# Late weights of a fused attention and two-MoE kernel: the bit operations of the float64 decode work in a PSUM bank instead of in place in SBUF

## Chip, cores and metric

The kernel runs on one core of a Trainium2 chip. The metric is the device time of one execution in microseconds (us). PE or TensorE is the matrix engine, DVE or VectorE, ACT or ScalarE, POOL or GpSimd and SP or SyncE are the others; SP issues the transfers here.

## What is computed

```python
# attention in chunks of 64 positions: batch 8, 8 heads, 576 positions, head dim 64
scores = scale * np.matmul(q_c, k_c.transpose(0, 1, 2, 4, 3))
scores = scores - np.max(scores, axis=-1, keepdims=True)
attn = np.exp(scores)
attn = attn / (np.sum(attn, axis=-1, keepdims=True) + 1e-09)
out = np.matmul(attn, v_c)
...
x = attn_out.transpose(0, 2, 1, 3).reshape(4608, 512)
h = x @ w_in                                # first MoE, 512 -> 2048 -> 512
x = (h * (1.0 / (1.0 + np.exp(-h)))) @ w_out
...
h = x @ w_in                                # second MoE, 512 -> 1024 -> 512
e = np.exp(h - np.max(h, axis=-1, keepdims=True))
solu = h * (e / (np.sum(e, axis=-1, keepdims=True) + 1e-09))
mu = np.mean(solu, axis=-1, keepdims=True)
var = np.mean((solu - mu) ** 2, axis=-1, keepdims=True)
out = ((solu - mu) / np.sqrt(var + 1e-06) * g_ln) @ w_out
```

## The kernel before

The 4608 tokens go through in nine blocks of 512. Each number is held as a pair of float16 values, a high part and the low rest, and a product of two such pairs is three matmuls into one PSUM bank. The helper `split` makes a pair: ScalarE writes the high part (L110), VectorE (L115) or GpSimd (L114) the low one. Blocks 0 and 1 use plain products (`h_group`, `x_part`, `m_h`, `m_out`), while the weights are still being decoded; later blocks use a scheme of seven products for each two-by-two block of operands (`h_fast`, `x_fast`, `m_fast`), whose operands `w1_sums` and `w2_sums` form from the weights during block 1 (lines 391 to 406).

The weights lie in DRAM as float64, that is as pairs of 32-bit words (tile `wst`). There are 48 of 128 x 512: numbers 0 to 31 are the first MoE's, 32 to 39 the second MoE's input weights `w3q`, 40 to 47 its output weights `w4h` and `w4l`. Each is decoded in three steps. `dec_scale` (L129, ScalarE) scales the high word as a float into a tile; `dec_bits` (VectorE) shifts the result left by 3 (L136), puts in three bits of the low word (L137) and the sign (L139); `dec_split` makes the pair, with GpSimd's low split for numbers up to 39 and VectorE's for 40 to 47. The order in which steps are handed over is

```python
    def weights(n=1):
        for _ in range(n):
            d3()
            d1()
            d2()
```

with `d1` the scaling of one weight, `d2` the bit operations and `d3` the split of an earlier one. Numbers below `SB = 32` are scaled into a PSUM bank `wp`, and only the last bit operation writes an SBUF tile `wy`. The 16 late weights, 32 to 47, are scaled straight into `wy` and worked on in place; they have two such buffers (pool `two`, tag `o`), so a scaling waits until the split of the weight two before has read its buffer. `NW1` and `NX1` say after which groups of block 1 `weights` is called.

All PSUM tiles come from one pool, `ps1`, of eight banks with one tag, taken in turn: hidden groups (`h_ps`, L362 to L364), attention scores and outputs (`s_ps`, `x_ps`), sums of weights (`wq`), `m_h`'s two banks (`h2_ps`, shown in traces as h_ps), and `wp`. A scheduler orders each engine's instructions by priority when the program is built; each engine then runs its own list in order. `m_h` of block 0 runs four times in block 1, before hidden groups 5, 7, 9 and 11, and `m_norm` follows it (L763 exp, L765 the product e, L771 square).

Of the kernel before, what the change touches and what calls it, by code (L numbers as in the profile page):

```python
# [10 lines left out]
I32 = mybir.dt.int32  # L11
AF = mybir.ActivationFunctionType
ALU = mybir.AluOpType
# [3 lines left out]
P = 128  # L17
# [29 lines left out]
def fused(ctx: ExitStack, tc: tile.TileContext, qkv, w1, w2, w3, w4, g_ln, out):  # L47
    nc = tc.nc
    V, A, G, T = nc.vector, nc.scalar, nc.gpsimd, nc.tensor
# [27 lines left out]
    ps1 = ctx.enter_context(tc.tile_pool(name="ps1", bufs=8, space=PSUM))  # L77
# [6 lines left out]
    for d in range(KD):  # L84
        for f in range(4):
            if f % 2 == 0:
                tag = f"w2_{2 * d + f // 2}" if d < 3 else f"q{12 + f // 2}"
                y = one.tile([P, 2, 2, 4, P], F16, tag=tag, name="w2t")
# [42 lines left out]
    def dec_bits(c, y):  # L131
        st, p, wh, wl, gain = c
        c[1] = y
        if y is None:
            c[1] = y = p
        V.tensor_scalar(out=p, in0=p, scalar1=3, scalar2=None, op0=ALU.logical_shift_left)  # L136
        V.scalar_tensor_tensor(out=p, in0=st[:, :, 0], scalar=29, in1=p,  # L137
                               op0=ALU.logical_shift_right, op1=ALU.bitwise_or)
        V.scalar_tensor_tensor(out=y, in0=st[:, :, 1], scalar=-2 ** 31, in1=p,  # L139
                               op0=ALU.bitwise_and, op1=ALU.bitwise_or)  # L140
# [228 lines left out]
    def g_split(b, f, eng_h=V):  # L369
        return split(*g_of(b, f), graw.pop(f), S_G, eng_h, V)  # L370
# [471 lines left out]
    for k in range(KD):  # L842
        for n in range(2):
            y = w3q[n, k // 2]
# [30 lines left out]
    def d2():  # L875
        if mid:
            i, c = mid.pop(0)
            dec_bits(c, ytile(i) if i < SB else None)
            out_.append((i, c))
            if at[0] < 36 or len(raw) + len(mid) < 2:  # L880
                fetch()
# [47 lines left out]
    for b in range(NB):  # L929
# [4 lines left out]
        for f in range(K1):  # L934
            if b < FAST:
# [10 lines left out]
                else:  # L946
                    y = g_split(b, f, A)
# [124 lines left out]
```

## Time and profile before

| | before |
|---|---|
| median of 3 runs | 1187.79 us (1187.39 to 1190.37) |
| profiled execution, its own time | 1187.17 us |
| its span | 1185.4 us |
| mean granted clock of TensorE | 0.986 |
| busy: TensorE, VectorE | 1130.4 us, 913.3 us |
| busy: ScalarE, GpSimd | 802.7 us, 250.6 us |

The span runs from the first to the last instruction of the profiled execution; its own time is a little longer. Busy shares are means over the whole span. Times of the trace below are microseconds from the start of the span.

### The profile page before, as it was taken

The page shows a single profiled execution, that of the slowest core. Times are in us where ns is not written, and L with a number is a line of the kernel's source. Part 1 is how long each engine was busy: PE and PEld are TensorE (multiplying, and loading weights), DVE is VectorE, ACT ScalarE, POOL GpSimd, SP SyncE. Part 2 cuts the span into 40 slices and gives each one's busy share as a digit, 9 for nine tenths or more (in the row PEclk, how much of TensorE's full clock was granted, in tenths as well). Part 3 has the DMA queues.
Part 4 walks back from the last instruction along what each step waited for, and adds up shares of the span by engine and source line. Part 5 has one row for each costly group of instructions (what it writes and reads, how often), then busy time and mean ns, then how long its engine had stood idle before and what let it go on. Part 6 is the DMA issues. An engine that isn't in the chain of part 4 may idle for free.

```text
span 1185.4 us, 23577 instructions
## 1 busy us (share of the span) xinstructions
PE 1130.4 (95%) x9036; PEld 767.9 (65%) x9036; DVE 913.3 (77%) x1638; ACT 802.7 (68%) x1475; POOL 250.6 (21%) x243
## 2 busy tenths in 40 slices
PE   5989998998999999999999999999999999999998
PEld 4434443444557866787678767876787777777863
DVE  5889999578587797789878986888689868886453
ACT  6787677775577667756875687568755875587243
POOL 2545424334201520031003100310021002100001
PEclk8989998999999999999999999999999999999999
DMA  7878554543346655777566667666777666655704
GB/s 276 269 233 253 176 180 107 161 145 123 125 116 196 187 178 153 187 206 196 160 187 198 195 159 196 196 197 160 170 216 203 160 161 213 179 161 133 208 25 115
DMA packets 205169, 209.18 MB, mean 176 GB/s; under 512 B 120192, under 2 KB 130432, under 8 KB 205056
## 3 DMA queue, kind: packets, MB, share of 16 engines
q1 hardware_dynamic: 205056, 207.68, 61.5%
q8 instruction: 70, 1.15, 0.4%
q14 instruction: 43, 0.35, 0.1%
HBM read 156.24 MB, written 24.12 MB: 152 GB/s over the span
## 4 chain that ended last, share of the span: by engine, by line
PE 52%; DVE 19%; ACT 11%; DMA 8%; issue 6%; POOL 2%; SPq 0%; ACTq 0%; POOLq 0%; DVEq 0%
PE o_ps L813 4%; PE o_ps L820 4%; PE o_ps L812 4%; PE pa L593 3%; PE pa L592 3%; PE pa L591 3%; PE pa L490 3%; DVE vbl L115 3%; PE pa L492 3%; PE pa L491 3%; DMA vs<-qkv 2%; DMA wst<-w 2%; DMA qk<-qkv 2%; PE pa L707 2%; DVE wy L139 2%
## 5 line engine op out<-in xcount | busy, mean ns | idle before, releaser
L110 ACT ACTIVATE q<-hc 128x512 f16<-128x512 f32 x196 | 119.1, 624 | 41.6 <-DVE hc L578 16.4
L115 DVE SCALAR_TENSOR_TENSOR q<-hc,q 128x512 f16<-128x512 f32 x196 | 138.2, 721 | 6.6 <-ACT q L110 5.1
L114 POOL TENSOR_TENSOR qbl<-qk,qbh 64x512 f16<-64x512 f32 x54 | 71.4, 1323 | 265.0 <-ACT qbh L110 222.6
L591 PE MATMUL pa<-q,ring 128*128 128x256 f16 x448 | 122.2, 273 | 0.0
L593 PE MATMUL pa<-q,ring 128*128 128x256 f16 x448 | 122.2, 273 | 0.0
L592 PE MATMUL pa<-q,ring 128*128 128x256 f16 x448 | 122.2, 273 | 0.0
L812 PE MATMUL o_ps<-w4h,uT 128*128 128x512 f16 x288 | 109.3, 380 | 0.3 <-ACT o L824 0.3
L813 PE MATMUL o_ps<-w4l,uT 128*128 128x512 f16 x288 | 109.3, 379 | 0.0
L778 POOL TENSOR_TENSOR c<-c,mhalf 128x2 f32<-128x2 f32 (+1 forms) x22 | 14.1, 640 | 393.1 <-DVE c L777 385.4
L491 PEld LDWEIGHTS <-ring 128*128 128x128 f16 x784 | 76.6, 98 | 19.6 <-issue 9.2
L592 PEld LDWEIGHTS <-ring 128*128 128x128 f16 x784 | 76.7, 98 | 11.1
L591 PEld LDWEIGHTS <-ring 128*128 128x128 f16 x784 | 76.6, 98 | 11.1
L490 PEld LDWEIGHTS <-ring 128*128 128x128 f16 x784 | 76.6, 98 | 10.5
L593 PEld LDWEIGHTS <-ring 128*128 128x128 f16 x784 | 76.6, 98 | 9.0
L492 PEld LDWEIGHTS <-ring 128*128 128x128 f16 x784 | 76.6, 98 | 9.0
L820 PE MATMUL o_ps<-w4h,uT 128*128 128x512 f16 x288 | 70.2, 379 | 0.0
L490 PE MATMUL pa<-x,ring 128*128 128x256 f16 x224 | 61.1, 273 | 7.7 <-ACT hc L512 5.0
L490 PE MATMUL pa<-xb,ring 128*128 128x256 f16 x224 | 61.1, 273 | 0.0
L491 PE MATMUL pb<-x,ring 128*128 128x256 f16 x224 | 61.1, 273 | 0.0
L492 PE MATMUL pb<-x,ring 128*128 128x256 f16 x224 | 61.1, 273 | 0.0
L492 PE MATMUL pa<-x,ring 128*128 128x256 f16 x224 | 61.1, 273 | 0.0
L591 PE MATMUL pb<-q,ring 128*128 128x256 f16 x224 | 61.1, 273 | 0.0
(277 smaller groups left out, 3493.1 us busy)
## 6 DMA issues: line engine op xcount, KB each, us to landing
ring<-w1s SPq DMA_DIRECT2D x196, 256.0 KB, 3.4
ring<-w2s SPq DMA_DIRECT2D x196, 256.0 KB, 3.6
wst<-w SPq DMA_DIRECT2D x48, 512.0 KB, 4.7
qk<-qkv SPq DMA_DIRECT2D x29, 512.0 KB, 3.7
vs<-qkv SPq DMA_DIRECT2D x36, 256.0 KB, 3.2
out<-o SPq DMA_DIRECT2D x36, 256.0 KB, 2.3
w1s<-ws SPq DMA_DIRECT2D x32, 128.0 KB, 1.7
w2s<-ws SPq DMA_DIRECT2D x16, 256.0 KB, 2.0
```

The source lines that it names most:

```text
L110: A.activation(dst_h, src, AF.Copy, scale=scale)
L114: return G.tensor_tensor(out=dst_l, in0=src, in1=dst_h, op=ALU.subtract).ins
L115: return V.scalar_tensor_tensor(out=dst_l, in0=src, scalar=scale, in1=dst_h, op0=ALU.mult, op1=ALU.subtract).ins
L490: T.matmul(ps[:, c], wh, x[:, 0, k], start=first, stop=False, skip_group_check=True)
L491: T.matmul(ps[:, c], wh, x[:, 1, k], start=False, stop=False, skip_group_check=True)
L492: T.matmul(ps[:, c], wl, x[:, 0, k], start=False, stop=k == 1, skip_group_check=True)
L591: T.matmul(ps[:, c], wh, g[:, 0], start=first, stop=False, skip_group_check=True)
L592: T.matmul(ps[:, c], wh, g[:, 1], start=False, stop=False, skip_group_check=True)
L593: T.matmul(ps[:, c], wl, g[:, 0], start=False, stop=q == 1 and f == 3, skip_group_check=True)
L812: T.matmul(ps, uh[:, k], w4h[:, k, :], start=k == 0, stop=False)
L813: T.matmul(ps, uh[:, k], w4l[:, k, :], start=False, stop=False)
L820: T.matmul(ps, ul[:, k], w4h[:, k, :], start=False, stop=k == K2 - 1)
```

## The change

For a late weight the shift now reads the SBUF tile that ScalarE has scaled, and writes a PSUM bank taken at this point, behind the scaling. The second operation works in that bank, and the third reads it and writes the same SBUF tile as before. These are 16 more PSUM tiles, one for each weight from 32 to 47. Weights below 32 are decoded as before. Lines behind 135 move down by two: L136, L137 and L139 become L138, L139 and L141, and `m_h`'s matmuls L663 become L665.

```diff
     def dec_bits(c, y):
         st, p, wh, wl, gain = c
         c[1] = y
+        s = p
         if y is None:
-            c[1] = y = p
-        V.tensor_scalar(out=p, in0=p, scalar1=3, scalar2=None, op0=ALU.logical_shift_left)
+            c[1] = y = s
+            p = ps1.tile([P, 512], I32, tag="mm", name="wp")
+        V.tensor_scalar(out=p, in0=s, scalar1=3, scalar2=None, op0=ALU.logical_shift_left)
         V.scalar_tensor_tensor(out=p, in0=st[:, :, 0], scalar=29, in1=p,
                                op0=ALU.logical_shift_right, op1=ALU.bitwise_or)
         V.scalar_tensor_tensor(out=y, in0=st[:, :, 1], scalar=-2 ** 31, in1=p,
                                op0=ALU.bitwise_and, op1=ALU.bitwise_or)
```

The order of TensorE's instructions is the same in both programs. Those of ScalarE and VectorE differ only where late weights are decoded. ScalarE, at the last attention tile of block 1, before (`wy_1386` is weight 32, `wy_1396` 33, `wy_1403` 34, `wy_1522` 35; `vbh` is the high part of v):

```order
L110 ACTIVATE x2_2_1432<-x2_ps_1329 128x512
L110 ACTIVATE vbh_115<-vs_1325 64x8x64 x2
L110 ACTIVATE x_1179<-x_ps_1435 128x4x128
L129 ACTIVATE wy_1396<-wst_1372 128x512
L110 ACTIVATE w3q_104<-wy_1386 128x512
L129 ACTIVATE wy_1403<-wst_1382 128x512
L110 ACTIVATE w3q_106<-wy_1396 128x512
L129 ACTIVATE wy_1522<-wst_1392 128x512
L110 ACTIVATE w3q_104<-wy_1403 128x512
L110 ACTIVATE x_1179<-x_ps_1493 128x4x128
```

and with the change, where `wy_1404` is weight 34 and `wy_1524` 35:

```order
L110 ACTIVATE x2_2_1434<-x2_ps_1329 128x512
L129 ACTIVATE wy_1396<-wst_1372 128x512
L110 ACTIVATE w3q_104<-wy_1386 128x512
L129 ACTIVATE wy_1404<-wst_1382 128x512
L110 ACTIVATE vbh_115<-vs_1325 64x8x64 x2
L110 ACTIVATE x_1179<-x_ps_1437 128x4x128
L110 ACTIVATE w3q_106<-wy_1396 128x512
L129 ACTIVATE wy_1524<-wst_1392 128x512
L110 ACTIVATE vbh_115<-vs_1466 64x8x64
L110 ACTIVATE x_1179<-x_ps_1495 128x4x128
```

The split of v stands behind the scalings of weights 33 and 34 now, where it stood ahead of both.

VectorE, around the bit operations of weight 40, before (`wy_1647` is weight 40, `wy_1656` 41; `g` is a hidden group's low half):

```order
L136 TENSOR_SCALAR wy_1647<-wy_1647 128x512
L137 SCALAR_TENSOR_TENSOR wy_1647<-wst_1625,wy_1647 128x512
L139 SCALAR_TENSOR_TENSOR wy_1647<-wst_1625,wy_1647 128x512
L115 SCALAR_TENSOR_TENSOR g_1642<-g_1640,g_1642 128x512
L136 TENSOR_SCALAR wy_1656<-wy_1656 128x512
L115 SCALAR_TENSOR_TENSOR w4l_109<-wy_1647,gs_110,w4h_108 128x512
L137 SCALAR_TENSOR_TENSOR wy_1656<-wst_1652,wy_1656 128x512
L139 SCALAR_TENSOR_TENSOR wy_1656<-wst_1652,wy_1656 128x512
```

and with the change (`wy_1654` with `wp_1666` is weight 40, `wy_1664` with `wp_1693` is 41; `wy_1626` is 39):

```order
L141 SCALAR_TENSOR_TENSOR wy_1626<-wst_1605,wp_1656 128x512
L115 SCALAR_TENSOR_TENSOR g_1649<-g_1647,g_1649 128x512
L138 TENSOR_SCALAR wp_1666<-wy_1654 128x512
L139 SCALAR_TENSOR_TENSOR wp_1666<-wst_1632,wp_1666 128x512
L138 TENSOR_SCALAR wp_1693<-wy_1664 128x512
L141 SCALAR_TENSOR_TENSOR wy_1654<-wst_1632,wp_1666 128x512
L139 SCALAR_TENSOR_TENSOR wp_1693<-wst_1660,wp_1693 128x512
L141 SCALAR_TENSOR_TENSOR wy_1664<-wst_1660,wp_1693 128x512
```

Weight 40's three operations stood together, and now weight 41's shift, which waits for weight 41's scaling, stands ahead of weight 40's last one.

TensorE at the first `m_h`, with the engine whose semaphore each instruction waits for, before:

```order
L663 LDWEIGHTS x2_0_1084
L663 MATMUL h2_ps_1751<-w3q_104,x2_0_1084 128x512 [waits DVE_49]
L663 LDWEIGHTS x2_0_1084
L663 MATMUL h2_ps_1752<-w3q_106,x2_0_1084 128x512 [waits Activation_49]
L663 LDWEIGHTS x2_0_1084
```

and with the change:

```order
L665 LDWEIGHTS x2_0_1084
L665 MATMUL h2_ps_1762<-w3q_104,x2_0_1084 128x512 [waits DVE_49]
L665 LDWEIGHTS x2_0_1084
L665 MATMUL h2_ps_1763<-w3q_106,x2_0_1084 128x512 [waits DVE_49]
L665 LDWEIGHTS x2_0_1084
```

The first two matmuls wait until their banks are free. Before, the first bank was last read by the low split of x2 and the second by a SiLU; now they were `wp` of weight 39 and of weight 40, last read by VectorE's L141. Likewise the second `m_h` has the banks of weights 43 and 44, the third that of weight 45 for its second matmul, and the fourth that of weight 46 for its first.

## Rows read from the trace of the kernel before

**Rows 1.** The page, part 1: busy us (share of the span) and instructions.

```profile
PE 1130.4 (95%) x9036; PEld 767.9 (65%) x9036; DVE 913.3 (77%) x1638; ACT 802.7 (68%) x1475; POOL 250.6 (21%) x243
```

**Rows 2.** Windows: length; busy us (instructions) of PE, PEld, DVE, ACT, POOL; granted clock; DMA.

```profile
160.00:170.00 10.00, 8.33 (x41) 3.88 (x40) 9.97 (x19) 6.32 (x13) 4.19 (x4) 1.00 0.67 220
170.00:180.00 10.00, 9.79 (x49) 4.58 (x47) 8.38 (x22) 9.18 (x17) 3.39 (x4) 1.00 0.50 156
...
188.00:190.00 2.00, 0.77 (x3) 0.22 (x3) 2.00 (x10) 1.55 (x2) 0.00 (x0) 0.61 0.00 0
190.00:192.00 2.00, 2.00 (x6) 0.74 (x5) 1.39 (x6) 1.88 (x3) 0.67 (x1) 0.50 0.00 0
192.00:194.00 2.00, 2.00 (x7) 0.92 (x6) 1.35 (x4) 2.00 (x7) 1.43 (x3) 0.50 0.19 66
194.00:196.00 2.00, 2.00 (x9) 0.80 (x7) 2.00 (x5) 1.23 (x2) 1.48 (x2) 0.68 0.38 131
```

**Rows 3.** Timeline, TensorE, 129 to 138 us: start, us, what, [idle before <-releaser].

```profile
129.57 0.20 PE L258 MATMUL x_ps<-pT,vbl 128*128 128x64 f16 x1 [0.64 <-DVE vbl L115]
...
136.83 0.38 PE L362 MATMUL h_ps<-x,w 128*128 128x512 f16 x1 [1.26 <-ACT x L110]
137.62 0.38 PE L363 MATMUL h_ps<-x,w 128*128 128x512 f16 x1 [0.41 <-DVE x L115]
```

**Rows 4.** Timeline, TensorE, 151 to 220 us.

```profile
151.22 0.81 PE L663 MATMUL h_ps<-w3q,x 128*128 128x512 f16 x3
...
162.45 0.81 PE L663 MATMUL h_ps<-w3q,x 128*128 128x512 f16 x3
...
169.46 0.38 PE L362 MATMUL h_ps<-x,w 128*128 128x512 f16 x1 [1.67 <-ACT g L366]
...
176.14 0.81 PE L663 MATMUL h_ps<-w3q,x 128*128 128x512 f16 x3
...
182.86 0.38 PE L362 MATMUL h_ps<-x,w 128*128 128x512 f16 x1 [1.37 <-ACT g L366]
...
188.93 0.37 PE L391 MATMUL wq<-w,ident 128*128 128x256 f16 x1 [2.89 <-DVE e L765]
...
195.30 0.60 PE L663 MATMUL h_ps<-w3q,x 128*128 128x512 f16 x2
...
219.31 0.38 PE L391 MATMUL wq<-w,ident 128*128 128x256 f16 x2 [0.94 <-DVE e L765]
```

**Rows 5.** Lines by form, VectorE, 100 to 240 us: count | busy us, mean ns | idle before.

```profile
L139 DVE SCALAR_TENSOR_TENSOR wy<-wst,wy 128x512 int32<-128x512 int32 x16 | 15.0, 935 | 0.3
L137 DVE SCALAR_TENSOR_TENSOR wy<-wst,wy 128x512 int32<-128x512 int32 x16 | 14.1, 878 | 0.3
...
L136 DVE TENSOR_SCALAR wy<-wy 128x512 int32<-128x512 int32 x16 | 7.6, 474 | 0.4 <-ACT wy L129 0.4
...
L139 DVE SCALAR_TENSOR_TENSOR wy<-wst,wp 128x512 int32<-128x512 int32 x7 | 4.8, 683 | 1.2 <-POOL w2t L114 1.0
...
L136 DVE TENSOR_SCALAR wp<-wp 128x512 int32<-128x512 int32 x6 | 4.2, 692 | 1.8 <-ACT wp L129 1.8
```

**Rows 6.** Timeline, VectorE, 130 to 170 us.

```profile
130.60 1.65 DVE L137 SCALAR_TENSOR_TENSOR wy<-wst,wy 128x512 int32<-128x512 int32 x1
...
154.32 0.69 DVE L139 SCALAR_TENSOR_TENSOR wy<-wst,wy 128x512 int32<-128x512 int32 x1
...
169.62 0.68 DVE L139 SCALAR_TENSOR_TENSOR wy<-wst,wy 128x512 int32<-128x512 int32 x1
```

**Rows 7.** Timeline, GpSimd, from 130 us.

```profile
130.56 1.15 POOL L114 TENSOR_TENSOR w3q<-wy,w3q 128x512 f16<-128x512 f32 x1 [2.33 <-ACT w3q L110]
```

**Rows 8.** Timeline, ScalarE, 127 to 154 us.

```profile
127.38 1.27 ACT L110 ACTIVATE vbh<-vs 64x512 f16<-64x512 f32 x2
...
131.74 0.69 ACT L129 ACTIVATE wy<-wst 128x512 f32<-128x512 f32 x1 [1.26 <-POOL w3q L114]
...
153.77 0.69 ACT L129 ACTIVATE wy<-wst 128x512 f32<-128x512 f32 x1 [0.15 <-POOL w3q L114]
```

## Prediction

> **What bounds the kernel now.** I read the page first: TensorE is busy for 95% of the span, VectorE for 77% [rows 1]. Over the whole run a shorter VectorE instruction is therefore worth nothing by itself; it counts only where TensorE waits. So I went to the stretch in which the late weights are decoded, about 122 to 200 us, and read windows: VectorE is full there (9.97 of 10 us from 160 to 170), and TensorE is not (8.33 of the same 10) [rows 2]. Then the timeline of TensorE, to see which wait ends last at each of its gaps: 0.64 us for the low half of v, 1.26 and 0.41 us for the last part of x [rows 3], and later 1.67, 1.37, 2.89 and 0.94 us for SiLU outputs and for m_norm's product e, which VectorE makes late because it is full [rows 4]. The 2.89 us gap costs more than itself: TensorE's granted clock is 0.61, 0.50, 0.50 and 0.68 in the four windows after 188 us, that is the lower level (1.2 of 2.4 GHz) for some 6 us; 0.77 x 0.39 + 2.0 x 0.5 + 2.0 x 0.5 + 2.0 x 0.32 = 2.9 us of matmul time are lost. After the 1.67 us gap at 169.46 the clock stayed at 1.00 [rows 2, 4].
>
> **The bit operations themselves.** 16 weights have three VectorE instructions each. With both tensors in SBUF, L139 took 15.0 us for 16 and L137 14.1 us; the form with one tensor in PSUM took 683 ns each [rows 5]. So 15.0 + 14.1 - 32 x 0.683 = 7.2 us are not work. What they are shows at 130.60: an L137 of 1.65 us beside a GpSimd split from 130.56 to 131.71 [rows 6, 7]. The change gives both two-input operations one SBUF input: -7.2 us. The shift reads SBUF and writes PSUM, which no row shows. Bounds: 474 ns, all in SBUF, and 692 ns, all in PSUM [rows 5]; nothing speaks for less than the first or more than the second. I take the second, since a PSUM operand is what the slower row has and the faster has not: 16 x 0.218 = +3.5 us. VectorE's sum is -3.7 us, and between -7.2 and -3.7 us by the bounds. The Trainium skill's page "VectorE: DVE Perf Modes", section "Why PSUM operands drop a tier", lets any fp32 operand in PSUM run at single rate only; by it the shift costs the same +3.5 us, and the sum stays.
>
> None of this reaches TensorE directly, because the weights' chain is bound by latency: scaling, bit operations, high split, low split, and the next scaling but one waits for that low split, over two SBUF buffers. ScalarE's scaling at 131.74 waited 1.26 us for GpSimd [rows 8]. The scalings from 131.74 to 153.77 are eight steps of 2.75 to 3.5 us, 22.03 in all. Buffers, splits and their waits are left as they were, so I leave the pace.
>
> **What the new order and the new banks do.** I walked the changed sequence with the durations of the rows; times are those of the trace before.
>
> A. v's split now stands on ScalarE behind the scalings of weights 33 and 34, and the latter waits for GpSimd's low split of weight 32. That split ran at 130.56 because its high split stood behind v; now it runs at about 129.55, ends at 130.7, the scaling takes 0.6 to the next start, and v begins at 131.3 instead of 127.38 [rows 7, 8]. Everything behind v keeps its distance, so the matmul at 129.57 [rows 3] starts at 133.5: **+3.9**. Queued behind v on ScalarE are two x splits; TensorE runs 5.3 us of other matmuls first, so x is then in time, and the gaps of 1.26 and 0.41 vanish: +3.9 - 1.67 = **+2.2** at the start of block 1.
>
> B. m_h now waits for banks that bit operations held. TensorE comes to the first m_h (151.22 [rows 4]) at about 153.4. Its second matmul needs the bank of weight 40, whose last operation ended at 154.32 + 0.69 [rows 6]. In the new order the shift of weight 41 stands ahead of it, and this waits for weight 41's scaling (153.77 [rows 8], and up to 1.3 later, since the splits ahead of it on ScalarE stand behind the SiLUs of a block that starts later). 153.8 to 155.1, 0.7 for the scaling, 0.7 each for the shift and the last operation: 155.9 to 157.2. I take 157.2: **+6.0**. Below, with no wait, it is +2.2.
>
> C. The second m_h (162.45) needs the banks of weights 43 and 44. From weight 40's to weight 44's last operation VectorE has 24 instructions in order, and it was full here before (9.97 of 10 [rows 2]); at the mean of that row (19 in 9.97 us) this is 12.6 us, 169.8, +7.3. The stretch has more of the 0.69 us operations than the row (eleven of the 24), and some wait for ScalarE's high splits, so I take 0.59 each, 14.2 us: 171.4, **+8.9**. Before, weight 44's last operation began at 169.62 [rows 6], so the wait is new only because the bank is. Then the 1.67 us gap falls away: +7.2.
>
> D. The third m_h (176.14) needs weight 45's bank, whose scaling stands on ScalarE behind the SiLU and split of the first hidden group after C. With that group at 179.3, SiLU, split and scaling (0.6, 0.6, 0.7), then the low half of g and three bit operations (0.6 and 3 x 0.7), each with up to 0.3 of hand-over, this ends between 183.9 and 185.4: **+9.2**; with no wait it is +7.2.
>
> E. From 176.14 to 195.30 there were 19.16 us, with gaps of 1.37 and 2.89 and the 2.9 us of clock. TensorE is now so late that VectorE and ScalarE are ahead of it there: 19.16 - 7.2 = 12.0, and the fourth m_h is at 185.4 + 12.0 = 197.4, +2.1 (up to +3.3 where it waits for weight 46's bank). I take **+3.0**. The 0.94 us gap at 219.31 [rows 4] is absorbed: **+2.0**. Behind it the sequences are the same, and I carry the delay to the end.
>
> A, B and D leave gaps of 2 to 4 us, which by the row of 2.89 can lower the clock; each such loss (2.9) ends in the next wait for a bank, which doesn't move with TensorE. I add nothing for it after the last.
>
> Sum: 1187.17 + 2.0 = 1189.2 on the profiled execution's own time (span 1185.4); the median of the runs shown, 1187.79, is 0.6 above it, so **1189.8 us**.
>
> **The rivals.** (1) Faster. The collisions decide and the bank waits are short. If the freed 7.2 us come out where VectorE is full, weights 40 to 46 end before TensorE asks, B to D cost nothing, and of the gaps of 1.37 and 2.89 and the clock's 2.9 (7.2 us) most is won: +2.2 - 1.67 - 7.2 + 2.9 for one clock loss behind A = -3.8, **1184.0 us**. For it: 1.65 beside 0.69 us in rows of one form; against: the pace was set by latency. It decides if weight 40 ends before 153.4. The Trainium skill's page "SBUF — State Buffer", section "SBUF: two separate sides", has a port pair that a VectorE instruction with two SBUF inputs and a reading GpSimd instruction hold in turn, the later blocking in full; by that rule all 7.2 us go, and the trace agrees at 130.60.
>
> (2) Clearly slower. The clock drops again after D, and weight 46's bank is late as well: 2.0 + 0.3 + 2 x 2.9 = +8.1, **1195.9 us**. For it: gaps of 2.89 lowered the clock; against: 1.67 didn't, and D's gap lies between.
>
> (3) It does nothing that lasts: later gaps absorb A to E, and nothing is won: **1187.8 us**. For it: a delay that carries to the end needs every later wait to move along.
>
> **How the numbers follow.** Chances: forecast 0.42, its own range 1187 to 1193; rival 1 0.24; rival 2 0.20; rival 3 0.14. 0.3% is 3.6 us, about what a measurement tells from no change: the bounds are 1184.2 and 1191.4. Faster: 0.20 of rival 1, and 0.02 of the forecast. Slower: 0.20 of rival 2 and 0.14 of the forecast. Within: the rest, 0.44. The range runs from rival 1 (with a little more won) to rival 2: 1183.3 to 1196.
>
> **What would show it.** The shift near 0.69 us and the two-input operations at no more than 0.70, with GpSimd running beside them. TensorE waiting some 4 us near 130 us for v; the m_h matmuls waiting for the last bit operation at about 157, 171 and 185; no gap near 189 and no clock of 0.50 there. Weight 40 done by 153 would refute B and speak for rival 1; a scaling of weight 41 well before 153 would show that the pace wasn't bound by latency. A gap behind 240 us that is smaller than before would mean that the delay is absorbed.

## The result: slower by 0.6 to 0.7%, 7 to 8 us

| | before | with the change |
|---|---|---|
| median of 5 runs each | 1187.39 us (1185.06 to 1190.37) | 1196.28 us (1193.07 to 1196.68) |
| ratio, 95% interval | 1 | 1.0068 [1.0054, 1.0083] |
| profiled execution, its span, mean granted clock | 1187.17 us, 1185.4 us, 0.986 | 1196.68 us, 1194.9 us, 0.986 |

The change is slower by more than the 0.3% that a measurement tells. By the ratio the time is 1187.79 x 1.0068 = 1195.9 us, at the upper end of the range (1196.0); the forecast of 1189.8 had the sign of the difference and a quarter of its size. The same kernel, measured again later, gave 1.0058 [1.0044, 1.0071], which is 6.9 us.

The page, part 1, of the changed kernel (busy us, share of the span, instructions) answers to [rows 1]:

```profile
PE 1128.9 (94%) x9036; PEld 769.4 (64%) x9036; DVE 910.4 (76%) x1638; ACT 802.3 (67%) x1475; POOL 249.9 (21%) x243
```

TensorE is busy 1.5 us less and VectorE 2.9 us less, and the weight loads, with 1.5 us more, lie beside matmuls; so TensorE is idle for 11.0 us more, the 9.5 us of span and the 1.5 us. The sum of VectorE was forecast at -3.7 us. VectorE's lines by form, 100 to 250 us, answer to [rows 5] (count | busy us, mean ns | idle before):

```profile
L139 DVE SCALAR_TENSOR_TENSOR wp<-wst,wp 128x512 int32<-128x512 int32 x23 | 15.7, 689 | 0.2
L141 DVE SCALAR_TENSOR_TENSOR wy<-wst,wp 128x512 int32<-128x512 int32 x23 | 15.6, 683 | 1.7 <-POOL w2t L114 1.1
...
L138 DVE TENSOR_SCALAR wp<-wy 128x512 int32<-128x512 int32 x16 | 11.0, 689 | 4.2 <-ACT wy L129 4.2
```

The bit operations do what was forecast: the two-input ones are down from 878 and 935 ns to 689 and 683, the shift from SBUF to PSUM is at 689. But the shift has 4.2 us of waits for ScalarE's scaling now, where [rows 5] has 0.4. What TensorE waits for between 110 and 260 us (total us, times, longest), the main entries of the view of waits:

```profile
PE h_ps L665 <- DVE wy L141: 7.9, 4, 3.2
PE x_ps L258 <- ACT vbh L110: 5.7, 1, 5.7
```

A third is 2.6 us for `kb`, the high part of keys of block 2. None of the three stands there before, with `vbh` at 0.45 us; in exchange the waits of 1.26, 1.67, 1.37 and 2.89 us of [rows 3, 4] are gone. Where they lie, TensorE's timeline (start, us, what, [idle before <-releaser]):

```profile
133.47 0.24 PE L258 MATMUL x_ps<-pT,vbh 128*128 128x64 f16 x1 [5.71 <-ACT vbh L110]
...
134.26 0.24 PE L260 MATMUL x_ps<-pT,vbl 128*128 128x64 f16 x1 [0.50 <-DVE vbl L115]
...
156.18 0.38 PE L665 MATMUL h_ps<-w3q,x 128*128 128x512 f16 x1
159.79 0.38 PE L665 MATMUL h_ps<-w3q,x 128*128 128x512 f16 x1 [3.23 <-DVE wy L141]
...
172.41 0.38 PE L665 MATMUL h_ps<-w3q,x 128*128 128x512 f16 x1 [1.44 <-DVE wy L141]
174.46 0.81 PE L665 MATMUL h_ps<-w3q,x 128*128 128x512 f16 x3 [1.68 <-DVE wy L141]
...
189.07 1.24 PE L665 MATMUL h_ps<-w3q,x 128*128 128x512 f16 x5 [1.52 <-DVE wy L141]
...
200.08 0.38 PE L665 MATMUL h_ps<-w3q,x 128*128 128x512 f16 x1
...
252.43 0.19 PE L213 MATMUL s_ps<-kb,qbh 128*128 128x64 f16 x1 [2.57 <-ACT kb L110]
253.22 0.19 PE L214 MATMUL s_ps<-kb,qbh 128*128 128x64 f16 x1 [0.60 <-DVE kb L115]
```

The lateness can be read off against [rows 3, 4]: +4.7 us at v (129.57 to 134.26), +5.0 at the first `m_h` (151.22 to 156.18), +4.8 at the fourth (195.30 to 200.08). Block 2's second score matmuls (L213, L214) wait at 252.43 and 253.22 for their keys, a place without any gap before; behind them it is +9.1 (a gap of 2.84 us for v is at 279.62 before, 288.69 now), and the end of the span is +9.5. So there are two places that cost: the 75 us around the late weights, and the keys.

**The first place: the pace.** ScalarE's timeline; L129 are the scalings, from that of weight 34 at 131.58:

```profile
131.58 0.66 ACT L129 ACTIVATE wy<-wst 128x512 f32<-128x512 f32 x1 [1.26 <-POOL w3q L114]
132.15 1.26 ACT L110 ACTIVATE vbh<-vs 64x512 f16<-64x512 f32 x2
...
157.76 0.66 ACT L129 ACTIVATE wy<-wst 128x512 f32<-128x512 f32 x1 [1.26 <-POOL w3q L114]
```

From weight 34 to 41 (eight scalings, so seven steps) it takes 157.76 - 131.58 = 26.2 us, against 22.0 in [rows 8]. VectorE's timeline in the same stretch shows the order that goes with it:

```profile
134.84 0.68 DVE L138 TENSOR_SCALAR wp<-wy 128x512 int32<-128x512 int32 x1
136.65 0.69 DVE L138 TENSOR_SCALAR wp<-wy 128x512 int32<-128x512 int32 x1 [1.12 <-ACT wy L129]
137.25 1.28 DVE L139 SCALAR_TENSOR_TENSOR wp<-wst,wp 128x512 int32<-128x512 int32 x2
...
139.47 1.27 DVE L141 SCALAR_TENSOR_TENSOR wy<-wst,wp 128x512 int32<-128x512 int32 x2
...
158.45 0.70 DVE L138 TENSOR_SCALAR wp<-wy 128x512 int32<-128x512 int32 x1 [0.76 <-ACT wy L129]
159.06 0.68 DVE L141 SCALAR_TENSOR_TENSOR wy<-wst,wp 128x512 int32<-128x512 int32 x1
```

Weights 34 and 35 go as a pair: both shifts, both L139, both L141. Weight 34 is scaled at 131.58 and done only behind 139.47, because the operations of weight 35, scaled at 135.95, stand between its own. Weights 36 and 37 go as a pair, too; 38 and 39 go one by one. The scaling of weight 38, the first behind the two pairs, is at 149.80, against 144.75 before (5.1 us late), and at weight 41 4.0 us are left of that. The same kind of order lies ahead of the first `m_h`: weight 40's L141, for whose bank TensorE waits until 159.79, stands behind weight 41's shift, and that behind weight 41's scaling of 157.76.

**The second place: the sums.** The high part of the keys stands on ScalarE behind the last split of `w1_sums` (tile `ws`). GpSimd's timeline with the change (`c` is `m_norm`'s, here of the fourth run):

```profile
224.13 0.55 POOL L780 TENSOR_TENSOR c<-c,mhalf 128x1 f32<-128x1 f32 x1 [10.05 <-DVE c L779]
224.76 2.82 POOL L114 TENSOR_TENSOR ws<-y,ws 128x256 f16<-128x256 f32 x3
...
251.15 0.67 POOL L114 TENSOR_TENSOR ws<-y,ws 128x256 f16<-128x256 f32 x1 [3.65 <-ACT ws L110]
```

and before:

```profile
214.82 2.36 POOL L114 TENSOR_TENSOR ws<-y,ws 128x256 f16<-128x256 f32 x3 [4.48 <-ACT ws L110]
...
221.97 0.55 POOL L778 TENSOR_TENSOR c<-c,mhalf 128x1 f32<-128x1 f32 x1 [1.72 <-DVE c L777]
...
242.09 0.67 POOL L114 TENSOR_TENSOR ws<-y,ws 128x256 f16<-128x256 f32 x1 [1.67 <-ACT ws L110]
```

Before, four low splits of the fifth group of sums ran ahead of the fourth `c`; now they stand behind it, GpSimd sits idle for 10.05 us ahead of `c`, and the last split of the sums is 9.1 us later, of which up to half may be TensorE's own lateness (4.6 us at block 2's first scores). Behind the second and third `c`, too, GpSimd has two and three splits that ran ahead of it before (8 and 12 are done there, and not 10 and 15).

This is not GpSimd's order alone. ScalarE makes the high parts of the same group. Its timeline before, where L763 is the exp of the fourth `m_norm`:

```profile
214.33 0.74 ACT L110 ACTIVATE ws<-y 128x256 f16<-128x256 f32 x2
...
217.75 0.69 ACT L763 ACTIVATE u<-h_ps,nm 128x512 f32<-128x512 f32 x1
```

and with the change, where the exp is L765:

```profile
219.38 0.69 ACT L765 ACTIVATE u<-h_ps,nm 128x512 f32<-128x512 f32 x1
...
224.28 1.01 ACT L110 ACTIVATE ws<-y 128x256 f16<-128x256 f32 x3
```

Before, 19 high parts of sums were made ahead of this exp, and now 16. The three others come at 224.28, behind `c`'s start at 224.13, so GpSimd could not have made their low parts earlier. So the sums are late on both engines, and ScalarE reaches the keys late:

```profile
250.66 0.42 ACT L110 ACTIVATE ws<-y 128x256 f16<-128x256 f32 x1 [3.50 <-DMA w1s<-ws]
...
251.75 0.63 ACT L110 ACTIVATE kb<-qk 128x512 f16<-128x512 f32 x1
```

The split at 250.66 waited for the transfer that empties an earlier `ws`, and `kb` came at once behind it. The change doesn't touch `w1_sums`; the scheduler, with other instructions ahead, has put GpSimd's and ScalarE's instructions in another order. The orders of ScalarE and VectorE differ up to about 236 us of the trace before, some 40 us behind the scaling of the last late weight (192.71), and not only where late weights are decoded.

### The profile page after: what moved, and what is told of

The parts are those of the page before. It is cut to its first block, busy times and chain, and to the rows that moved or that the text cites. A ratio compares the mean times of both kernels' runs of the same rounds, so it can differ in the third digit from the quotient of the medians.

```text
span 1194.9 us, 23594 instructions
## 1 busy us (share of the span) xinstructions
PE 1128.9 (94%) x9036; PEld 769.4 (64%) x9036; DVE 910.4 (76%) x1638; ACT 802.3 (67%) x1475; POOL 249.9 (21%) x243
## 4 chain that ended last, share of the span: by engine, by line
PE 60%; DVE 12%; ACT 9%; DMA 8%; issue 6%; POOL 3%; SPq 0%; ACTq 0%; DVEq 0%; POOLq 0%
PE o_ps L822 5%; PE o_ps L815 5%; PE o_ps L814 5%; PE pa L595 3%; PE pa L594 3%; PE pa L593 3%; PE pa L492 3%; PE pa L494 3%; PE pa L493 3%; DMA wst<-w 3%; DVE vbl L115 2%; PE pa L711 2%; PE pa L710 2%; PE pa L709 2%; DMA vs<-qkv 2%
## 5 line engine op out<-in xcount | busy, mean ns | idle before, releaser
L492 PE MATMUL pa<-x,ring 128*128 128x256 f16 x224 | 61.5, 274 | 7.3 <-ACT hc L514 4.8
L494 PE MATMUL pa<-x,ring 128*128 128x256 f16 x224 | 61.6, 275 | 0.0
L493 PE MATMUL pa<-x,ring 128*128 128x256 f16 x224 | 61.5, 275 | 0.0
L492 PE MATMUL pa<-xb,ring 128*128 128x256 f16 x224 | 61.1, 273 | 0.0
L493 PE MATMUL pa<-xb,ring 128*128 128x256 f16 x224 | 61.1, 273 | 0.0
L494 PE MATMUL pa<-xb,ring 128*128 128x256 f16 x224 | 61.1, 273 | 0.0
```

Source lines behind the costliest of these rows:

```text
L492: T.matmul(ps[:, c], wh, x[:, 0, k], start=first, stop=False, skip_group_check=True)
L493: T.matmul(ps[:, c], wh, x[:, 1, k], start=False, stop=False, skip_group_check=True)
L494: T.matmul(ps[:, c], wl, x[:, 0, k], start=False, stop=k == 1, skip_group_check=True)
```

## The experiments

The theory after the result is the prediction's own: the late v and `m_h`'s waits for banks of bit operations cost the time. The rivals: the bit operations in PSUM are slower as a whole (then they cost without the banks' waits, too); the loss lies in GpSimd's order and the keys alone; the loss is one of these waits alone. Several kernels share the runs of the kernel before that were taken with them.

**1. One bank of their own for the bit operations.** The late `wp` come from a pool of one PSUM bank, and seven are left for the rest, so that no `m_h` inherits one. The edit is to the changed kernel.

```diff
-    ps1 = ctx.enter_context(tc.tile_pool(name="ps1", bufs=8, space=PSUM))
+    ps1 = ctx.enter_context(tc.tile_pool(name="ps1", bufs=7, space=PSUM))
+    psw = ctx.enter_context(tc.tile_pool(name="psw", bufs=1, space=PSUM))
...
-            p = ps1.tile([P, 512], I32, tag="mm", name="wp")
+            p = psw.tile([P, 512], I32, tag="wl", name="wp")
```

> The bit operations of the late weights go through one PSUM bank of their own, and the other tiles have seven banks. m_h then takes no bank from a bit operation, and v's split stands on ScalarE behind the scaling of weight 33 only. If the waits of m_h for bit operations (7.9 us in the changed kernel's trace) and the order of v's split (5.7 us) are the loss, this is within 3 us of the kernel before or faster by up to 4 us (the 7.2 us of collisions less 3.4 us of slower shifts), with no m_h wait for L141's successor. If the loss came from the bit operations in PSUM themselves, or from sums of weights that come late on GpSimd and SyncE, it stays 6 to 9 us slower.

Measured: 1186.99 us against 1185.94, ratio 1.0011 [1.0000, 1.0023].

**2. Its control: the kernel before with seven banks.**

```diff
-    ps1 = ctx.enter_context(tc.tile_pool(name="ps1", bufs=8, space=PSUM))
+    ps1 = ctx.enter_context(tc.tile_pool(name="ps1", bufs=7, space=PSUM))
```

> Control: the kernel before with seven PSUM banks, late weights in place in SBUF. If a bank less costs nothing, 0 to 2 us slower than the kernel before; if banks are short in the decoding stretch, 3 us slower or more, and then the run with a bank of its own is to be held against this one.

Measured: 1186.38 us, 1.0000 [0.9983, 1.0018]. What `m_h` waits for in the kernel with the bank of its own, in the view of waits:

```profile
PE h_ps L666 <- ACT g L369: 6.1, 2, 3.9
```

and its last bit operation, in VectorE's lines by form:

```profile
L142 DVE SCALAR_TENSOR_TENSOR wy<-wst,wp 128x512 int32<-128x512 int32 x22 | 15.1, 685 | 2.1 <-POOL w2t L115 1.1
```

No `m_h` waits for a bit operation; it waits 6.1 us for SiLUs (7.8 us in the control), and that costs nothing against eight banks. The operations are as short as in the change (685 ns), so VectorE is freed of the collisions, and neither kernel is faster than the one before. This refutes the rival that the operations in PSUM are slower as a whole: nearly all of the 0.7% is gone. It refutes the prediction's rival 1 just as well. What it doesn't do is to take away the shared banks alone: with one bank no two weights can be interleaved, and the scalings of weights 34 to 41 take 22.5 us, about as before, and not the 26.2 of the change; TensorE waits 3.2 us for v's high part and not 5.7; and GpSimd and ScalarE have the sums of the fifth group in their old places.

**3. and 4. One half of the weights each.** Only weights 40 to 47, or only 32 to 39, get the bank. Against the change; `gain` is set for weights 40 to 47, and the other kernel has `gain is None`.

```diff
         if y is None:
             c[1] = y = s
+        if y is s and gain is not None:
             p = ps1.tile([P, 512], I32, tag="mm", name="wp")
```

> Only weights 40 to 47 go through PSUM. v's split stands on ScalarE as before; of the four m_h only the first takes a bank that a bit operation held (weight 40's). If the order of v's split is the main loss, within 2 us of the kernel before; if the bank waits of m_h are, 3 to 5 us slower; if late sums of weights are, 4 us slower or more with the split of keys waited for near 250 us.

> Only weights 32 to 39 go through PSUM. v's split stands behind two scalings as in the change, and no m_h takes a bank that a bit operation held. If the order of v's split is the main loss, 4 to 6 us slower than the kernel before; if the bank waits of m_h are, 0 to 2 us slower, since TensorE makes up for the late v at gaps of 1.67 and 1.26 us.

Measured: weights 40 to 47 alone 1188.9 us, 1.0020 [1.0005, 1.0035]; weights 32 to 39 alone 1185.56, 0.9993 [0.9981, 1.0005]. TensorE's timeline of the latter:

```profile
134.22 0.23 PE L259 MATMUL x_ps<-pT,vbh 128*128 128x64 f16 x1 [6.25 <-ACT vbh L110]
...
155.87 4.48 PE L666 MATMUL h_ps<-w3q,x 128*128 128x512 f16 x20
...
190.42 0.27 PE L394 MATMUL wq<-w,ident 128*128 128x256 f16 x1 [2.97 <-DVE e L768]
```

The late v costs 6.25 us here, and the first `m_h` is 4.6 us late (155.87, without a wait); yet the fourth is at 195.8, as before: the gaps of 1.67 and 1.37 us are not there, and that in front of L394 was 2.89 before. So v late by itself costs nothing, and neither does the slow pace: the scalings from 132.33 to 158.53 take 26.2 us, as in the change. With weights 40 to 47 alone (by the ratio 2.4 us slower, between the ranges that were expected) v comes with a wait of 1.31 us, the first `m_h` waits 1.20 us for weight 40, and the keys are 2.75 + 0.61 us late. Neither half costs 0.7%, nor do both together (0.9993 and 1.0020).

**5. and 6. The sums' low splits off GpSimd.** Four low splits of the fifth group of `w1_sums` go to VectorE, in the change and, as a control, in the kernel before.

```diff
-            split(z[:, 0], z[:, 1], y, 1.0, A, G)
+            split(z[:, 0], z[:, 1], y, 1.0, A, V if 17 <= sn[0] <= 20 else G)
```

> The changed kernel, with the four low splits of w1_sums' fifth group (the one that stood on GpSimd behind the fourth m_norm's c) on VectorE. All banks and waits of m_h are as in the change. If the late sums of weights on GpSimd are a cause of their own, the waits for the keys' splits near 252 us (2.57 and 0.60 us) go, and it is 3 to 5 us faster than the change, that is 3 to 6 us slower than the kernel before. If all of the loss is m_h's bank waits, it stays 8 us slower, and the keys' wait stays or is taken by another.

> Control: the same move of four low splits to VectorE in the kernel before. No keys' wait stood there, so within 1.5 us of the kernel before by either theory.

Measured: 1192.32 us against 1187.08, 1.0042 [1.0025, 1.0058]; the control 1.0004 [0.9990, 1.0017]. The keys' wait falls from 2.57 to 0.97 us, `m_h`'s waits for bit operations stay at 7.9. Against the change's 1.0068 [1.0054, 1.0083] the intervals just overlap, so this run alone only suggests that the sums are part of the loss; more than half is left. The keys' wait was expected to go and did not: ScalarE's high parts of this group still stand behind the fourth exp (from 223.1 us).

**7. Only weights 43 to 47 in banks.** No v is moved, and the first `m_h` finds no bank of a bit operation. `cnt` counts the weights. Against the change:

```diff
+    cnt = [-1]
...
         s = p
+        cnt[0] += 1
         if y is None:
             c[1] = y = s
+        if y is s and cnt[0] in range(43, 48):
             p = ps1.tile([P, 512], I32, tag="mm", name="wp")
```

> Only weights 43 to 47 go through PSUM. v's split is in its old place, the first m_h has its old banks, and the second to fourth m_h take banks of weights 43 to 46 as in the change; GpSimd has the changed order, c ahead of four low splits. If the loss is the bank waits of the later m_h and the late sums, 4 to 8 us slower than the kernel before. If it needs TensorE to be late at the first m_h (late v, weight 40's bank), 0 to 3 us slower.

Measured: 1191.22 us against 1187.08, 1.0031 [1.0019, 1.0042], by the ratio 3.7 us, between the two ranges. TensorE's timeline at the second `m_h`:

```profile
166.83 0.38 PE L669 MATMUL h_ps<-w3q,x 128*128 128x512 f16 x1 [3.35 <-DVE wy L145]
168.89 1.44 PE L669 MATMUL h_ps<-w3q,x 128*128 128x512 f16 x3 [1.68 <-DVE wy L145]
```

With 1.30 at the third these waits are 6.3 us, but the fourth `m_h` is at 195.3, where it was before: the gaps of 1.37 and 2.89 take them up. What this kernel loses it loses behind that, the keys' wait of 1.75 + 0.60 us among it.

**8. The bank taken ahead of the scaling.** In the kernel before, all weights are scaled into a bank.

```diff
-    SB = 32
+    SB = 48
```

> All 48 weights as the early ones: ScalarE scales into a PSUM bank, VectorE shifts there. The bank is taken ahead of the scaling. Each of the four m_h waits for one bit operation (weights 40, 44, 46, 47), and GpSimd has the changed order. If bank waits and late sums are the loss, 4 to 9 us slower than the kernel before; if the two SBUF buffers that the scaling waits for are, since this needs none until the last operation, it is not slower.

Measured: 1193.93 us against 1187.08, 1.0053 [1.0034, 1.0072]. `m_h` waits for the last bit operation again (the view of waits):

```profile
PE h_ps L663 <- DVE wy L139: 8.1, 2, 5.9
```

This kernel has v nearly in time (a wait of 1.98 us) and the keys' wait at 0.60 us, so by this trace it owes little of its loss to either. Two of the four `m_h` wait for bit operations, where all four were expected to. Long waits of `m_h` for bit operations come without the change's order of v. That they alone make up the loss isn't shown, since the kernel differs in other places, too.

**9. GpSimd's new order at the fourth `c` alone.** In the kernel before, the four low splits are held behind the fourth `c`, as the change has them; the second and third `c` and ScalarE's order ahead of the exp (19 high parts) stay as they were.

```diff
-            split(z[:, 0], z[:, 1], y, 1.0, A, G)
+            A.activation(z[:, 0], y, AF.Copy)
+            with tc.issue_after(cs[3]) if 17 <= sn[0] <= 20 else nullcontext():
+                G.tensor_tensor(out=z[:, 1], in0=y, in1=z[:, 0], op=ALU.subtract)
...
+    cs = []
...
-        G.tensor_tensor(out=c, in0=c, in1=mhalf.to_broadcast([P, n]) if n > 1 else mhalf, op=ALU.pow)
+        cs.append(G.tensor_tensor(out=c, in0=c, in1=mhalf.to_broadcast([P, n]) if n > 1 else mhalf, op=ALU.pow).ins)
```

> The kernel before (late weights in place in SBUF), with one order forced on GpSimd: the four low splits of w1_sums' fifth group stand behind the fourth m_norm's c, as in the change. No m_h waits for a bit operation. If the late sums are a cause of their own, the keys' splits are waited for near 245 us and it is 2 to 5 us slower than the kernel before; if they only matter when TensorE is late already, within 1 us.

Measured: 1187.55 us against 1184.57, 1.0022 [1.0012, 1.0032], by the ratio +2.6 us. TensorE's timeline shows the keys' wait in a kernel in which no weight is touched:

```profile
247.02 0.19 PE L211 MATMUL s_ps<-kb,qbh 128*128 128x64 f16 x1 [1.09 <-ACT kb L110]
247.81 0.19 PE L212 MATMUL s_ps<-kb,qbh 128*128 128x64 f16 x1 [0.60 <-DVE kb L115]
```

So late low splits by themselves cost time, and the keys' wait goes with them. The loss is under the 0.3% named above, but its interval stands above 1, and the two controls and the kernel before again lie between 0.9993 and 1.0004. Of the kernels with banks, those with 16 or 15 high parts ahead of the fourth exp are all at 1.0020 or more (the change and its two versions, weights 40 to 47, 43 to 47, and experiment 8), and those with 19 at 1.0011 or less (bank of their own, weights 32 to 39). Banks for weights from 43 on and ScalarE's new order come together in these kernels, so this alone doesn't show which of the two costs.

**10. and 11. Eight low splits to VectorE, and the change again beside it.** The first is experiment 5 with more splits moved; the second differs from the change by an empty line.

```diff
-            split(z[:, 0], z[:, 1], y, 1.0, A, G)
+            split(z[:, 0], z[:, 1], y, 1.0, A, V if 17 <= sn[0] <= 24 else G)
```

> The changed kernel with eight low splits (the fifth and sixth group of w1_sums) on VectorE. If what was left of the keys' wait with four of them (0.97 and 0.60 us) is the same chain of sums, it goes to 0.6 us or less and the kernel is 3 to 5 us slower than before; if VectorE has become late by the added work, it is 5 us slower or more.

> The changed kernel once more, on the same chip as the two others: 7 to 9 us slower than the kernel before, with m_h's four waits for bit operations (about 8 us) and the keys' waits (about 3 us) again. If the 1.2 us by which its trace was late at 110 us, ahead of the first late weight, belongs to the change, it is there again; if it is scatter, it is not.

Measured against 1184.57: eight splits 1191.09, 1.0047 [1.0034, 1.0060], by the ratio 5.6 us, and so above the first of the two ranges, keys 0.66 + 0.60; the change 1191.65, 1.0058 [1.0044, 1.0071]. Its gaps in TensorE's timeline, whose first one ends 2.6 us earlier than in the first trace:

```profile
130.85 0.23 PE L258 MATMUL x_ps<-pT,vbh 128*128 128x64 f16 x1 [5.56 <-ACT vbh L110]
...
156.80 5.70 PE L665 MATMUL h_ps<-w3q,x 128*128 128x512 f16 x13 [3.24 <-DVE wy L141]
171.47 0.81 PE L665 MATMUL h_ps<-w3q,x 128*128 128x512 f16 x3 [0.38 <-DVE wy L141]
186.07 6.16 PE L665 MATMUL h_ps<-w3q,x 128*128 128x512 f16 x20 [3.21 <-DVE wy L141]
248.83 0.19 PE L213 MATMUL s_ps<-kb,qbh 128*128 128x64 f16 x1 [1.67 <-ACT kb L110]
```

The waits are the same in kind; the second `m_h` waits 0.38 us only. What moving the low splits gives back is 1.0068 - 1.0042 in one set and 1.0058 - 1.0047 in the other, 1.3 to 3 us, and the intervals overlap. Experiment 9 makes it 2.6 us. So the share of the sums is some 2 us, and not settled more closely: ScalarE's part of the new order is in both versions still.

**12. The kernel before again**, with two blank lines more, for the scatter between traces.

> The kernel before once more (two blank lines in it), for a second trace. If the stages that the comparison uses hold, from the third attention tile of block 1 (122.2 us) to the fourth m_h 73 us and from there to the second scores of block 2 62 to 63 us, each within 1.5 us; if they scatter by more, differences of that size between traces mean nothing.

Measured: 1186.67 us against 1188.3, 0.9993 [0.9976, 1.0009]. The second stage holds, at 62.8 us; the first is 70.9 and not 73.1 us, more than the 1.5 us that were allowed. So a difference of some 2 us in the first stage of two single traces means nothing.

**All traces side by side.** Lengths of two stages, in us from the starts of instructions in TensorE's timeline. Stage 1 runs from the first output matmul of block 1's third attention tile (122.2 before) to the fourth `m_h`, stage 2 from there to block 2's third scores (257.9 before; the expectation above calls them the second). The three waits are TensorE's for v's high part, of `m_h` for the last bit operation, and for the keys. The last two columns are parts of stage 1: TensorE's idle time, and the matmul time lost to the lower clock (its busy time at that clock, times one less the granted clock).

| kernel | ratio | v | m_h | keys | stage 1 | stage 2 | idle in 1 | clock in 1 |
|---|---|---|---|---|---|---|---|---|
| before | 1 | 0.4 | 0 | 0 | 73.1 | 62.6 | 9.2 | 3.0 |
| before again | 0.9993 | 1.9 | 0 | 0 | 70.9 | 62.8 | 8.3 | 1.7 |
| seven banks | 1.0000 | 2.3 | 0 | 0 | 73.5 | 65.3 | 9.7 | 3.6 |
| four sums on VectorE, before | 1.0004 | 1.0 | 0 | 0.5 | 70.8 | 66.0 | 9.8 | 0 |
| late sums | 1.0022 | 2.1 | 0 | 1.7 | 72.0 | 67.0 | 9.6 | 1.6 |
| bank of their own | 1.0011 | 3.2 | 0 | 0.6 | 70.4 | 66.6 | 7.7 | 3.1 |
| weights 32 to 39 | 0.9993 | 6.3 | 0 | 0 | 73.8 | 63.6 | 10.5 | 3.1 |
| weights 40 to 47 | 1.0020 | 1.3 | 1.2 | 3.4 | 71.9 | 67.1 | 7.0 | 4.7 |
| weights 43 to 47 | 1.0031 | 0.4 | 6.3 | 2.4 | 73.5 | 65.1 | 10.1 | 2.8 |
| change | 1.0068 | 5.7 | 7.9 | 3.2 | 78.4 | 67.6 | 14.5 | 3.6 |
| change again | 1.0058 | 5.6 | 6.8 | 2.3 | 79.5 | 63.6 | 12.9 | 6.7 |
| change, four sums on VectorE | 1.0042 | 4.6 | 7.9 | 1.6 | 78.5 | 62.9 | 12.9 | 5.6 |
| change, eight sums on VectorE | 1.0047 | 5.6 | 7.6 | 1.3 | 78.0 | 64.0 | 13.6 | 4.5 |
| bank ahead of the scaling | 1.0053 | 2.0 | 8.1 | 0.6 | 79.7 | 64.2 | 13.7 | 5.7 |

Stage 1 falls into two sets with nothing between: 70.4 to 73.8 us, and 78.0 to 79.7. The second set holds the change in all its versions and the kernel with a wait of 5.9 us at the third `m_h`. Less idle time and less the clock's loss, the stage is 59.6 to 61.0 us in every trace, so the sets differ by these two: idle time is 7.0 to 10.5 us in the first and 12.9 to 14.5 in the second, the clock's loss 0 to 4.7 and 3.6 to 6.7. A late v alone (6.3) is in the first set, and so are waits of `m_h` alone at 6.3 us; there the idle time is hardly more than before, since the waits have taken the place of other gaps. I read this as one reserve, the gaps of the kernel before in this stage (1.67 + 1.37 + 2.89 us, and the clock's loss, which is 3.0 us in one trace of it and 1.7 in the other): it takes up one of the two delays, and neither both nor the 8.1 us and the 1.62 us for e of the kernel with the bank ahead of the scaling. Waits of `m_h` for SiLUs, which the column leaves out, fit in: within stage 1 the kernels with seven banks and with a bank of their own have 5.4 and 3.9 us of them, so both kinds of delay come to 7.7 and 7.1 us there, in the first set. This is a reading of one trace for each kernel. Stage 2 has no such sets: 62.6 to 67.6, with 65.3 and 66.0 where the keys wait 0 and 0.5 us. No kernel beats the one before.

## Why the prediction came out as it did

**The bit operations: right.** The shift was taken at 0.692 us and has 0.689; the two-input forms were to be at most 0.70, and the longest is 0.701. The Trainium skill's page "SBUF — State Buffer", section "SBUF: two separate sides", holds here too, as far as the rows go: with one SBUF input there is no row above 0.701 us, GpSimd's splits running beside. The forecast of the sum, -3.7 us, is what these rows give; VectorE's busy time as a whole is down by 2.9. What follows for the time is another matter: the kernel with a bank of its own has the short operations and not the waits, at 1.0011 against 1.0000 of its control. That the freed VectorE time doesn't reach TensorE was the right judgement, and rival 1 is refuted.

**A: right in kind, a little small.** v's split began at 132.15, not 131.3, because GpSimd's split of weight 32 ran at 130.39 and not 129.55; the matmul is +4.7 and not +3.9. That the gaps of 1.26 and 0.41 vanish holds. But TensorE was at the first `m_h` at 156.18, not 153.4: besides the 0.8, the 5.71 us gap lowered its clock. The windows (length, busy us, count, clock, DMA share, GB/s) answer to [rows 2]:

```profile
134.00:136.00 2.00, 1.74 (x24) 0.50 0.81 241
136.00:138.00 2.00, 2.00 (x7) 0.57 0.24 87
```

At the lower level 1.74 x 0.5 + 2.0 x 0.43 = 1.7 us of matmul time are lost. The prediction named this loss and left it out, since a bank that doesn't move with TensorE would end it.

**B: the step that failed first.** "Buffers, splits and their waits are left as they were, so I leave the pace": the pace went from 22.0 to 26.2 us for seven steps (of 2.5 to 3.5 us before; the prediction counted eight). The two pairs of weights 34 to 37 come with it: with a bank of their own, where there are no pairs, the steps take 22.5 us, and with weights 32 to 39 in banks, where the pairs are, 26.2; v's split stands in another place in the two as well. Weight 41's scaling, forecast at 153.8 to 155.1, is at 157.76, and weight 40's bank is free at 159.79 and not 157.2. The rows to see it by were in front of me: the order of VectorE around weight 40 already shows the shift of the next weight ahead of the last operation of this one. I priced it there, for one weight, and not for weights 34 to 37. How much of the 2.6 us at weight 40's bank is the pairs and how much the later hidden groups wasn't separated.

**C, D and E: right, as distances, within 2 us.** From weight 40's bank to the second `m_h`'s last bank was forecast 171.4 - 157.2 = 14.2 us and is 174.46 - 159.79 = 14.7; from there to the third 14.0, and is 14.6; from the third to the fourth 12.9 (185.4 to 195.3 + 3.0), and is 11.0. In the second trace of the change the three are 14.7, 14.6 and 12.7. The gap near 189 for m_norm's e is gone, as said. The low clock behind it is gone in the first trace; in the second the clock is at 0.65 and 0.50 from 186 to 190, behind the third `m_h`'s wait of 3.21 us. The lateness at the fourth `m_h` in the first trace, +4.8 where I had +3.0, is the 2.6 us of B and these three differences (0.5 + 0.6 - 1.9).

**The end: the step that failed most.** "Behind it the sequences are the same, and I carry the delay to the end": forecast +2.0, measured +9.5 in the profiled execution. At block 2's first scores it is still +4.6 (234.1 before, 238.6 now). Then come the keys, 2.57 + 0.60 us, and behind that gap the clock:

```profile
254.00:256.00 2.00, 2.00 (x9) 0.50 0.81 221
256.00:258.00 2.00, 2.00 (x8) 0.70 0.14 49
```

2.0 x 0.5 + 2.0 x 0.30 = 1.6 us. Together 4.8 us, about the step from +4.6 to +9.1. I had taken the orders of ScalarE and VectorE to differ only where late weights are decoded, and never looked at GpSimd's. All three differ behind that, ScalarE's at the sums' high parts, which came ahead of the fourth exp before and come behind it now. The late-sums kernel shows that late low splits alone cost 0.22%; what ScalarE's order costs beside it has no run of its own. How the 4.8 us of this one trace divide between the sums and TensorE's own lateness stays open: with the low splits moved the whole is 1.3 to 3 us less.

**The rivals.** Rival 2's price, 1195.9, is what was measured, and the time lies within the range (by 0.1 us) only because the range ends at this price. That is luck: in the first trace behind D the clock is 1.00 (190 to 192 us), and the fourth `m_h` waits for no bank. In the second trace the clock does fall behind D, but the fourth `m_h` again waits for no bank, and the keys, which take 2.3 to 4.8 us in the two, stand in neither the forecast nor rival 2. Rival 3, that later gaps absorb it all, is what happens where only v is late (weights 32 to 39). I had given the two waits separate terms and added what was left; as I read the table, the gaps behind them are one reserve (some 7 us behind the second `m_h`: 1.37 + 2.89 and the clock's 2.9), which pays for one and is then spent.

Not tried: the change with v's split in its old place and all else as it is, and the change with ScalarE's old order at the sums. The first would show whether the bank waits alone, at their size in the change, fill stage 1; the kernel with the bank ahead of the scaling, with v in time and other waits, is the nearest to it.

## What to carry to other kernels

A scratch tile taken from a rotating pool makes its next user wait for the last reader of the scratch: before moving work into a shared bank, list who gets each bank next, and when its last reader can be done. When a change makes a scheduler order anew, compare the orders of all engines up to the point where they agree again, also far behind the edit and on the engine with the least work; here the sums of weights, which the edit doesn't touch, came late on ScalarE and on GpSimd, an engine busy for 21% of the span, and with them the keys. And count on a gap that absorbs one delay to absorb that one only: subtract what each delay takes up from one common reserve.

## What the runs showed of the hardware that was not expected

The length of a gap alone didn't tell whether TensorE's clock falls. Behind the 3.23 us gap at 159.79 the granted clock stayed at 1.00, while it fell to 0.50, the lower level (1.2 of 2.4 GHz), behind 2.89 us in [rows 2, 4], and behind the two short gaps of 1.44 and 1.68 us, which stand 2 us apart (windows of the change: length, busy us, count, clock, DMA share, GB/s):

```profile
160.00:162.00 2.00, 2.00 (x11) 1.00 0.53 135
...
176.00:178.00 2.00, 2.00 (x6) 0.50 0.85 320
```

Not even the same gap at the same place decides it. In the second trace of the change the wait of 3.24 us for the same bank, up to 156.80, let the clock fall to 0.50, and in the kernel before with four sums on VectorE the gap of 2.89 us for e, up to 188.22, left it at 1.00 (windows in the order of [rows 2]). The change again:

```profile
158.00:160.00 2.00, 2.00 (x6) 0.73 (x5) 1.78 (x4) 2.00 (x4) 0.00 (x0) 0.50 0.87 260
```

The kernel before with four sums on VectorE:

```profile
190.00:192.00 2.00, 2.00 (x12) 1.04 (x11) 1.62 (x4) 2.00 (x6) 0.76 (x2) 1.00 0.19 66
```

So the clock's loss is no fixed part of a kernel's time: in stage 1 it is 3.0 and 1.7 us in two traces of the kernel before, and 3.6 and 6.7 us in two of the change. What decides it, no run here was made to find out. Traces of the same kernel differ, too: the third attention tile of the kernel before begins at 122.2 us in one and 125.1 in another, so that a difference of 2 us in the place of one instruction of one trace says little.
